# Logits with tokens first from three 16-bit parts, blank entries in order, the first expert tiles' steps earlier, V ahead of the first scores

## The chip, the cores and the metric

The kernel runs on one core of a Trainium2 chip. The metric is the device time of one execution in microseconds; a smaller time is better. A core has a matrix engine (TensorE, PE in the profile, with its weight loads as PEld), VectorE (DVE), ScalarE (ACT), GpSimd (POOL) and SyncE (SP), which here issues DMAs; GpSimd issues DMAs too, the indirect ones among them. Each engine runs its own instructions in order, and they wait for each other by semaphores.

## The reference

Eight batches of attention without softmax, gated by `u`, whose output feeds a mixture of 8 experts, one expert for each token:

```
scores = (1 / S) * z @ z.T                # z: 8 x 2496 x 64
x = u * (max(scores, 0) ** 2 @ v)         # u, v, x: 8 x 2496 x 256
x = x.reshape(19968, 256)
logits = x @ w_gate                       # 256 x 8
e = argmax(logits); gate = softmax(logits)[e]
out = gate * (max(x @ w1[e], 0) @ w2[e])  # w1: 8 x 256 x 1024, w2: 8 x 1024 x 256
```

All data are 32-bit floats, and results must be near those of 32-bit arithmetic.

## The kernel before

**Numbers in parts.** TensorE multiplies in a shorter 32-bit format (`fp32r`). An operand `a` is therefore held as two parts, `hi`, which is `a` copied to that format, and `lo = a - hi`, and a product is three matmuls: hi x hi, hi x lo and lo x hi. The copy is a ScalarE instruction (sometimes VectorE), the subtraction a VectorE one.

**Attention** (`scores`, `weighted`). A batch has 5 chunks of queries (512, the last 448) and 20 blocks of 128 keys, taken in pairs, so that a step `s` is one batch, one chunk and one pair of key blocks: 8 x 5 x 10 = 400 steps. For a step, `scores` makes the 256 x 512 block of squared scores: four matmuls into PSUM (L299, L300), relu and square on ScalarE (L301, L302), then hi (L304) and lo (L306). The score matrix is symmetric, so a block below the diagonal is not computed again: the block above it is turned (L267), written to DRAM as `scr` (L270) and brought back later by four loads (`bring`, L277), at steps that a planner fixes up to `AHEAD = 8` steps ahead of the use. `weighted` then multiplies with V's two parts into two PSUM accumulators: 12 matmuls (L325, L327, L328). `scores` runs `LA = 3` steps ahead of `weighted`. V is loaded by key pair (`fetch_v`, L138) into four buffers and split by `split_v` (ScalarE copy L143, subtraction L145 on VectorE or, in batch 0 from the third pair on, GpSimd). In batch 0 z and V arrive while the first chunk runs.

**After each chunk** (`gate_x`). VectorE forms `x = acc * scale * u` with the 256 features on partitions and tokens along the free side (L350), then hi on ScalarE (L352) and lo on VectorE (L353). Two pieces of work go on the list `bg`, which the main loop takes from, one a step, from the third step of the next chunk on: `logits` and `turn_rows` (x turned to rows and written to DRAM, L365, L370). `logits` has the gate weights as the stationary operand: `wg2` holds for each half of the features 8 columns hi and 8 columns lo, padded to 32, and x streams past, hi and lo, 4 matmuls of 512 columns (L377). Their result has the 32 columns on partitions and tokens along the free side; four 32-row transposes on VectorE (L382) bring tokens to partitions, and `choose` adds the two halves (L405). `route` then picks the expert (`choose`), takes exponentials (`exps`, L401) and finds each token's place among its expert's (`place`: five small 16-bit matmuls L426, L428, then eight VectorE instructions). Four indirect DMAs (L445) scatter entries (gate, token number) into the list `lst` in DRAM, which has a region for each expert.

**Blank entries.** A region is filled with entries that name a pad token before the tokens' own entries come. `blank(b, h)` writes half a batch's share, 624 KB in runs of 768 bytes (L233). Batch 0's two blanks, the regions' ends (L221) and the spare rows (L223) are issued by GpSimd in `constants`; the blanks of batch `b + 1` by SyncE, called at steps 5 and 8 of batch `b`'s second chunk.

**Order.** Instructions are written in program order, but the framework's scheduler may move an instruction ahead on its engine when nothing that it depends on forbids it. `pinned(work)` forbids that: the work's instructions stay behind the last one of each engine at that point. `declare_no_dep` says of two accesses of one DRAM tensor that they touch different places and need not wait for each other.

**Experts.** `tile_list` turns the counts into tiles of 512, 384 or 256 tokens of one expert. Six tiles, the list "A", are built from the counts of the first seven batches, so that they can start while the last batch is routed; the others form the list "F". For a tile, `load_e` fetches its entries (L659), `load_x` its rows (L670), `turn_x` turns them (L700) and passes them through DRAM (`far`, L703, L705), `split_x` makes hi and lo (L715, L716); `load_w` fetches expert weights (L644) and `split_piece` splits them (L689 to L692). `up` and `down` are the two products (L733; L754, L756), and `finish` scatters the result (L767). For the first tiles these calls hang on the last steps of the attention: `loads` names them by their distance from the last step, with `NKP = 10` steps a chunk.

Of the kernel before, what the change touches and what calls it, by code (L numbers as in the profile page):

```python
# [19 lines left out]
P = 128  # L20
# [3 lines left out]
E = 8  # L24
# [24 lines left out]
def fused_kernel(ctx: ExitStack, tc: tile.TileContext, zt, ut, v, wg, wcat, out):  # L49
# [121 lines left out]
    wg2 = const.tile([P, 2, R], FR, name="wg2")  # L171
# [34 lines left out]
    def constants():  # L206
        nc.vector.memset(wg2.bitcast(F32), 0.0)
        nc.vector.tensor_copy(wg2[:, :, 0:E], wg_sb)
        nc.vector.tensor_tensor(wg2[:, :, E:2 * E], wg_sb, wg2[:, :, 0:E].bitcast(F32), op=ALU.subtract)
        for ti, tf in iotas:  # L210
# [7 lines left out]
        blank(0, 0, nc.gpsimd)  # L218
        blank(0, 1, nc.gpsimd)
        w = BIG * ENT // P  # L220
        nc.gpsimd.dma_start(regions[:, NTOK * ENT:].rearrange("e (p k) -> p e k", k=w),  # L221
                            pad[:, 0:w].unsqueeze(1).broadcast_to([P, E, w]))
        nc.gpsimd.dma_start(lst[NROW * SMALL:].rearrange("(p r) k -> p (r k)", p=P), pad[:, 0:w])  # L223

    regions = lst[0:E * CAP].rearrange("(e c) k -> e (c k)", e=E)
    blanks, scatters = [], []

    def blank(b, h, eng=None):
# [4 lines left out]
        i = (eng or nc.sync).dma_start(regions[:, at:at + n * w].rearrange("e (p k) -> p e k", k=w),  # L233
# [108 lines left out]
    def gate_x(b, c, acc):  # L342
# [4 lines left out]
        xh = sb.tile([P, 2, QC], FR, name="xh")  # L347
        xl = sb.tile([P, 2, QC], FR, name="xl")
# [3 lines left out]
        nc.scalar.copy(xh[:, :, :n], x[:, :, :n])  # L352
        nc.vector.tensor_tensor(xl[:, :, :n], x[:, :, :n], xh[:, :, :n].bitcast(F32), op=ALU.subtract)  # L353
# [4 lines left out]
        lw = sb.tile([P, QC // P, R], F32, name="lw", bufs=2)  # L358
        if n < QC:
            nc.gpsimd.memset(lw[n % P:P, ns - 1], 0.0)  # L360
# [11 lines left out]
        def logits():  # L372
            pt = psm.tile([P, QC], F32, name="pt", tag="psm")
            m = 0
            for i in range(2):
                for xx in (xh, xl):
                    nc.tensor.matmul(pt[0:R, :n], lhsT=wg2[:, i], rhs=xx[:, i, :n], start=m == 0, stop=m == 3)  # L377
                    m += 1
            for g in range(G):
                w = -(-(n - g * R) // P)  # L380
                src = pt[0:R].rearrange("p (s g k) -> p g s k", g=G, k=R)[:, g, 0:w]
                nc.vector.transpose(out=lw[g * R:(g + 1) * R, 0:w], in_=src)  # L382
# [3 lines left out]
        lazy.extend(route(b * S + q0, n, ns, lw, gw))  # L386
# [4 lines left out]
    def route(t0, n, ns, lw, gw):  # L391
# [11 lines left out]
        def choose():  # L403
            l = sb.tile(sh, F32, name="l", bufs=2)
            nc.vector.tensor_tensor(l, lw[:, 0:ns, 0:E], lw[:, 0:ns, E:2 * E], op=ALU.add)  # L405
# [14 lines left out]
        def place():  # L420
# [22 lines left out]
            for j in range(ns):  # L443
# [206 lines left out]
    def load_e(i):  # L650
# [7 lines left out]
        for src, at, a, z in parts:  # L658
            nc.gpsimd.indirect_dma_start(out=to[:, a * ENT:z * ENT], out_offset=None, in_=src,  # L659
                                         in_offset=bass.IndirectOffsetOnAxis(ap=eidx[:, at:at + 1], axis=0))  # L660
# [159 lines left out]

    for b in range(B):
        for c in range(NC_):
            s0 = (b * NC_ + c) * NKP
            at(s0 + 2, lambda b=b, c=c: fetch_u(b, c))
            if c == 1 and b + 1 < B:
                for h in range(2):
                    at(s0 + 5 + 3 * h, lambda b=b, h=h: blank(b + 1, h))
# [5 lines left out]
        for kp in range(NKP):  # L833
            if b:
# [162 lines left out]
```

## Time and profile before

| | |
|---|---|
| time, median of 3 runs | 2303.61 us (2300.22 to 2307.38) |
| time of the profiled execution | 2306.15 us |
| its span, first to last instruction | 2304.4 us |
| mean granted TensorE clock | 0.989 |
| busy: TensorE matmuls, VectorE, ScalarE, GpSimd | 97%, 72%, 59%, 29% |
| DMA | 414.28 MB, mean 180 GB/s |

The attention takes the span's first 1364 us, the experts the rest. In the timelines a row gives start, duration, engine, line, operation, tiles (out<-in), shapes and count, and in brackets the idle time of the engine before it with what ended that. In the groups by line a row gives the count, total busy time and mean nanoseconds of one, then the idle time before them. A matmul's duration includes its passage through the array, so matmuls overlap, and the distance of their starts tells their cost.

### The profile page before, as it was taken

The numbers are of one execution on the slowest core, as the hardware profiler recorded it, in microseconds if no ns is written. First come the engines' busy times: TensorE is split into PE (matmuls) and PEld (weight loads), VectorE is DVE, ScalarE is ACT, GpSimd is POOL, SyncE is SP. The second block draws the span as 40 slices with busy tenths as digits, with TensorE's granted clock in tenths as the row PEclk, the third lists the DMA queues.
The fourth block names the chain that finished last, engine by engine and source line by source line (L and its number), as shares of the span: only waits on it lengthen the run. The fifth ranks groups of instructions, "written<-read, shape, count | busy, mean of one in ns | idle before, by whom it ended". The sixth has DMA issues, their size and how long they took to land. (4 is left out here: it accounts for less than half of the span.)

```text
span 2304.4 us, 31091 instructions
## 1 busy us (share of the span) xinstructions
PE 2233.8 (97%) x10864; PEld 1864.5 (81%) x10864; DVE 1653.1 (72%) x2798; ACT 1368.1 (59%) x1818; POOL 673.9 (29%) x724
## 2 busy tenths in 40 slices
PE   5999999999999999999999989999999999999997
PEld 3788788788888888887887878888888888888886
DVE  5687887887887888878878767566566675666653
ACT  4667757857768658667667643454454454554543
POOL 2210020120120120210220344545445555545521
PEclk8999999999999999999999999999999999999999
DMA  8865774775666756657657674555465556556520
GB/s 263 248 183 146 220 191 138 221 178 172 202 162 181 222 141 195 194 142 230 178 129 215 188 225 140 193 166 183 136 200 187 185 186 193 180 164 223 180 87 22
DMA packets 247180, 414.28 MB, mean 180 GB/s; under 512 B 105539, under 2 KB 146056, under 8 KB 227558
## 3 DMA queue, kind: packets, MB, share of 16 engines
q1 hardware_dynamic: 214006, 291.08, 44.1%
q0 software_dynamic: 33008, 121.12, 16.5%
q8 instruction: 87, 1.43, 0.3%
q14 instruction: 79, 0.65, 0.1%
HBM read 254.55 MB, written 158.07 MB: 179 GB/s over the span
## 5 line engine op out<-in xcount | busy, mean ns | idle before, releaser
L325 PE MATMUL acc<-thi,t 128*128 128x512 f32 (+1 forms) x1200 | 453.8, 389 | 23.8 <-ACT t L143 21.2
L328 PE MATMUL acc<-thi,t 128*128 128x512 f32 (+1 forms) x1200 | 462.3, 388 | 0.9 <-POOL t L145 0.5
L445 POOL DMA_INDIRECT lst<-gw,posi x160 | 172.6, 1078 | 963.9 <-DVE posi L442 468.0
L327 PE MATMUL acc<-tlo,t 128*128 128x512 f32 (+1 forms) x1144 | 444.4, 389 | 0.9 <-DVE tlo L306 0.5
L737 ACT ACTIVATE t<-ph 128x512 fp32r<-128x512 f32 (+1 forms) x328 | 192.5, 588 | 342.2 <-PE ph L733 262.0
L733 PE MATMUL ph<-thi,t 128*128 128x512 f32 (+2 forms) x1248 | 377.8, 362 | 14.7 <-ACT thi L715 9.2
L738 DVE SCALAR_TENSOR_TENSOR t<-ph,t 128x512 fp32r<-128x512 f32 (+1 forms) x328 | 220.5, 674 | 229.8 <-ACT t L737 190.6
L754 PE MATMUL y<-t,t 128*128 128x512 f32 x1062 | 379.3, 397 | 1.7 <-DVE tf L765 1.4
L301 ACT ACTIVATE tf<-ps_s 128x1024 f32<-128x1024 f32 (+1 forms) x240 | 242.2, 1017 | 231.5 <-PE ps_s L300 224.5
L756 PE MATMUL y<-t,t 128*128 128x256 f32 x1062 | 290.0, 281 | 2.3 <-DVE t L738 2.3
L325 PEld LDWEIGHTS acc<-thi,t 128*128 128x128 f32 x1200 | 226.3, 189 | 71.3 <-ACT t L143 24.0
L733 PEld LDWEIGHTS ph<-thi,t 128*128 128x128 f32 x1248 | 226.4, 190 | 52.5 <-ACT thi L715 9.3
L328 PEld LDWEIGHTS acc<-thi,t 128*128 128x128 f32 x1200 | 226.8, 189 | 43.9 <-POOL t L145 1.9
L302 ACT ACTIVATE tf<-tf 128x1024 f32<-128x1024 f32 (+1 forms) x240 | 250.4, 1053 | 4.6
L327 PEld LDWEIGHTS acc<-tlo,t 128*128 128x128 f32 x1144 | 216.7, 189 | 42.9 <-DVE tlo L306 3.5
L306 DVE TENSOR_TENSOR tlo<-tf,thi 128x1024 fp32r<-128x1024 f32 (+1 forms) x168 | 203.6, 1215 | 62.0 <-ACT thi L304 59.4
L754 PEld LDWEIGHTS y<-t,t 128*128 128x128 f32 x1062 | 198.0, 188 | 44.7 <-DVE tf L765 1.8
L267 DVE STREAM_TRANSPOSE s<-tf 128x1024 f32<-128x1024 f32 x160 | 197.5, 1235 | 47.1 <-ACT tf L302 42.7
L733 PE MATMUL ph<-tlo,t 128*128 128x512 f32 (+2 forms) x624 | 225.7, 362 | 2.2 <-issue 1.5
L767 POOL DMA_INDIRECT out_dram<-tf,ent x160 | 165.6, 1035 | 184.5 <-DVE tf L765 125.0
L756 PEld LDWEIGHTS y<-t,t 128*128 128x128 f32 x1062 | 200.5, 189 | 14.8 <-DVE t L738 3.7
L670 POOL DMA_INDIRECT rows<-xrows,ent x160 | 164.5, 1028 | 107.5 <-DMA ent<-lst,lfeidx 64.9
(238 smaller groups left out, 3962.7 us busy)
## 6 DMA issues: line engine op xcount, KB each, us to landing
scr<-s SPq DMA_DIRECT2D x80, 1024.0 KB
s<-scr SPq DMA_DIRECT2D x320, 256.0 KB
vr<-in_v_dram SPq DMA_DIRECT2D x80, 256.0 KB
u<-in_ut_dram SPq DMA_DIRECT2D x32, 512.0 KB
xrows<-th SPq DMA_DIRECT2D x128, 128.0 KB
far<-th SPq DMA_DIRECT2D x31, 512.0 KB
th<-far SPq DMA_DIRECT2D x124, 128.0 KB
zr<-in_zt_dram SPq DMA_DIRECT2D x36, 256.0 KB
```

Source lines behind the costliest of these rows:

```text
L267: nc.vector.transpose(out=to, in_=a.rearrange("p i (t s k) -> p i t s k", t=4, s=G))
L301: nc.scalar.activation(a[:, :, :n], ps[:, :, :n], AF.Relu)
L302: nc.scalar.activation(a[:, :, :n], a[:, :, :n], AF.Square)
L306: nc.vector.tensor_tensor(lo[:, :, :n], a[:, :, :n], hi[:, :, :n].bitcast(F32), op=ALU.subtract)
L325: nc.tensor.matmul(acc[d][:, :n], lhsT=vh, rhs=hi[:, i, :n], start=first and i == 0, stop=False)
L327: nc.tensor.matmul(acc[d][:, :n], lhsT=vh, rhs=lo[:, i, :n], start=False, stop=False)
L328: nc.tensor.matmul(acc[d][:, :n], lhsT=vl, rhs=hi[:, i, :n], start=False, stop=last and i == 1)
L733: nc.tensor.matmul(o, lhsT=w1[:, part, dd, fs], rhs=xx[:, dd, :n], start=p == 0, stop=p == 5)
L737: nc.scalar.activation(hh[:, :m], ph[:, :m], AF.Relu)
L738: nc.vector.scalar_tensor_tensor(hl[:, :m], ph[:, :m], 0.0, hh[:, :m].bitcast(F32), op0=ALU.max, op1=ALU.subtract)
L754: nc.tensor.matmul(y, lhsT=hh[:, cs], rhs=w2[:, f % 2].rearrange("p i d -> p (i d)"), start=f == 0, stop=False)
L756: nc.tensor.matmul(y[:, 0:D], lhsT=hl[:, cs], rhs=w2[:, f % 2, 0, :], start=False, stop=f == NF - 1)
```

## The change

Four parts.

1. **Logits.** x is split into three 16-bit parts that sum to it: the upper halves of x's 32-bit words, read in place at every second 16-bit element (`tops[0]`), the upper halves of what remains (`x1`, `tops[1]`), and the rest of that as a 16-bit tile (`x2`). Both subtractions are VectorE's; ScalarE's copy is gone. The parts are the stationary operand, 128 tokens at a time, and the gate weights in three 16-bit parts side by side (24 columns) stream past. A chunk has 4 blocks of tokens x 2 halves of the features x 3 parts = 24 matmuls, whose result has tokens on partitions; one VectorE sum over the three weight parts (two for a chunk of 448) gives `l`. The transposes, `lw` and the addition in `choose` are gone.
2. **Blanks.** All are issued by SyncE and pinned: batch 0's at steps 6 and 7, the regions' ends and spare rows (`tails`) at step 8, the later ones at the places where they were called.
3. **First expert tiles.** Entry loads of the list "A" and the scatters of the last batch are declared free of each other, and the first tiles' calls are moved: `load_e(0)`, `load_e(1)`, `load_x(0)`, `load_e(2)`, `load_x(1)` and `turn_x(0)` by 4, 4, 2, 8, 4 and 3 steps.
4. **V in the first chunk.** The split of the next key pair's V is emitted ahead of `scores` of three steps later, instead of behind it.

```diff
     def constants():
-        nc.vector.memset(wg2.bitcast(F32), 0.0)
-        nc.vector.tensor_copy(wg2[:, :, 0:E], wg_sb)
-        nc.vector.tensor_tensor(wg2[:, :, E:2 * E], wg_sb, wg2[:, :, 0:E].bitcast(F32), op=ALU.subtract)
+        for k in range(3):
+            nc.vector.tensor_copy(wg3[:, :, k, :], wg_sb)
+            if k < 2:
+                nc.vector.tensor_tensor(wg_sb, wg_sb, wg3[:, :, k, :], op=ALU.subtract)
...
-        blank(0, 0, nc.gpsimd)
-        blank(0, 1, nc.gpsimd)
+
+    def tails():
+
         w = BIG * ENT // P
-        nc.gpsimd.dma_start(regions[:, NTOK * ENT:].rearrange("e (p k) -> p e k", k=w),
-                            pad[:, 0:w].unsqueeze(1).broadcast_to([P, E, w]))
-        nc.gpsimd.dma_start(lst[NROW * SMALL:].rearrange("(p r) k -> p (r k)", p=P), pad[:, 0:w])
+        nc.sync.dma_start(regions[:, NTOK * ENT:].rearrange("e (p k) -> p e k", k=w),
+                          pad[:, 0:w].unsqueeze(1).broadcast_to([P, E, w]))
+        nc.sync.dma_start(lst[NROW * SMALL:].rearrange("(p r) k -> p (r k)", p=P), pad[:, 0:w])
...
-        xh = sb.tile([P, 2, QC], FR, name="xh")
-        xl = sb.tile([P, 2, QC], FR, name="xl")
+        x1 = sb.tile([P, 2, QC], F32, name="x1")
+        x2 = sb.tile([P, 2, QC], BF16, name="x2")
+        tops = [t.bitcast(BF16).rearrange("p i (n h) -> p i n h", h=2)[:, :, :, 1] for t in (x, x1)]
...
-        nc.scalar.copy(xh[:, :, :n], x[:, :, :n])
-        nc.vector.tensor_tensor(xl[:, :, :n], x[:, :, :n], xh[:, :, :n].bitcast(F32), op=ALU.subtract)
+        nc.vector.tensor_tensor(x1[:, :, :n], x[:, :, :n], tops[0][:, :, :n], op=ALU.subtract)
+        nc.vector.tensor_tensor(x2[:, :, :n], x1[:, :, :n], tops[1][:, :, :n], op=ALU.subtract)
...
         def logits():
             pt = psm.tile([P, QC], F32, name="pt", tag="psm")
-            m = 0
-            for i in range(2):
-                for xx in (xh, xl):
-                    nc.tensor.matmul(pt[0:R, :n], lhsT=wg2[:, i], rhs=xx[:, i, :n], start=m == 0, stop=m == 3)
-                    m += 1
-            for g in range(G):
-                w = -(-(n - g * R) // P)
-                src = pt[0:R].rearrange("p (s g k) -> p g s k", g=G, k=R)[:, g, 0:w]
-                nc.vector.transpose(out=lw[g * R:(g + 1) * R, 0:w], in_=src)
+            W = 3 * E
+            for t in range(ns):
+                m = min(P, n - t * P)
+                for i in range(2):
+                    for xx in (*tops, x2):
+                        nc.tensor.matmul(pt[:m, t * W:(t + 1) * W], lhsT=xx[:, i, t * P:t * P + m],
+                                         rhs=wg3[:, i].rearrange("p k e -> p (k e)"),
+                                         start=t == 0 and i == 0 and xx is tops[0],
+                                         stop=t == ns - 1 and i == 1 and xx is x2, skip_group_check=True)
+            sums = pt[:, 0:ns * W].rearrange("p (t k e) -> p t e k", k=3, e=E)
+            full = n // P
+            nc.vector.tensor_reduce(l[:, 0:full], sums[:, 0:full], axis=AX.X, op=ALU.add)
+            if full < ns:
+                nc.vector.tensor_reduce(l[:n % P, full], sums[:n % P, full], axis=AX.X, op=ALU.add)
...
         def choose():
-            l = sb.tile(sh, F32, name="l", bufs=2)
-            nc.vector.tensor_tensor(l, lw[:, 0:ns, 0:E], lw[:, 0:ns, E:2 * E], op=ALU.add)
...
+                for o in firsts:
+                    tc.declare_no_dep(i.ins, o.ins, reason="places of an earlier batch")
...
+            if which == "A":
+                firsts.append(d)
+                for of, o in scatters:
+                    if of == B - 1:
+                        tc.declare_no_dep(d.ins, o.ins, reason="places of a later batch")
...
+    for h in range(2):
+        at(6 + h, lambda h=h: pinned(lambda: blank(0, h)))
+    at(8, lambda: pinned(tails))
...
-                    at(s0 + 5 + 3 * h, lambda b=b, h=h: blank(b + 1, h))
+                    at(s0 + 5 + 3 * h, lambda b=b, h=h: pinned(lambda: blank(b + 1, h)))
...
-    loads = {NKP + 4: [lambda: load_e(0)],
-             NKP + 3: [lambda: load_e(1)],
-             NKP + 2: [lambda: load_x(0)],
+    loads = {2 * NKP - 2: [lambda: load_e(0)],
+             2 * NKP - 3: [lambda: load_e(1)],
+             NKP + 4: [lambda: load_x(0)],
+             NKP + 3: [lambda: load_e(2)],
              NKP + 1: [lambda: load_w(0, 0)],
+             NKP: [lambda: load_x(1)],
              NKP - 1: [lambda: load_w(0, 1)],
              NKP - 3: [lambda: load_w(1, 0)],
-             NKP - 4: [lambda: load_x(1)],
-             NKP - 5: [lambda: turn_x(0), lambda: load_e(2)],
+             NKP - 2: [lambda: turn_x(0)],
              1: [lambda: load_x(2), lambda: load_e(3)],
              0: [lambda: turn_x(1)]}
...
+        if s < NKP and kp + 1 < NKP:
+            pinned(lambda: split_v(0, kp + 1))
         if s + LA <= LAST:
             ready[s + LA] = scores(*steps[s + LA])
-        if s < NKP:
-            if kp + 1 < NKP:
-                pinned(lambda: split_v(0, kp + 1))
-            if kp % 2 == 0 and kp // 2 + 2 < NC_:
-                pinned(lambda: split_z(0, kp // 2 + 2))
+        if s < NKP and kp % 2 == 0 and kp // 2 + 2 < NC_:
+            pinned(lambda: split_z(0, kp // 2 + 2))
```

More of the change, by code (lines that the diff above doesn't have):

```diff
@@ L170, in fused_kernel @@
     make_identity(nc, ident)
-    wg2 = const.tile([P, 2, R], FR, name="wg2")
+    wg3 = const.tile([P, 2, 3, E], BF16, name="wg3")
     wg_sb = const.tile([P, 2, E], F32, name="wg_sb")
@@ L217, in constants, with blank @@
         nc.gpsimd.iota(pad.bitcast(I32)[:, 1:PAD * ENT:ENT], pattern=[[0, PAD]], base=NTOK, channel_multiplier=0)
-        blank(0, 0, nc.gpsimd)
-        blank(0, 1, nc.gpsimd)
+    def tails():
         w = BIG * ENT // P
-        nc.gpsimd.dma_start(regions[:, NTOK * ENT:].rearrange("e (p k) -> p e k", k=w),
-                            pad[:, 0:w].unsqueeze(1).broadcast_to([P, E, w]))
-        nc.gpsimd.dma_start(lst[NROW * SMALL:].rearrange("(p r) k -> p (r k)", p=P), pad[:, 0:w])
+        nc.sync.dma_start(regions[:, NTOK * ENT:].rearrange("e (p k) -> p e k", k=w),
+                          pad[:, 0:w].unsqueeze(1).broadcast_to([P, E, w]))
+        nc.sync.dma_start(lst[NROW * SMALL:].rearrange("(p r) k -> p (r k)", p=P), pad[:, 0:w])
     regions = lst[0:E * CAP].rearrange("(e c) k -> e (c k)", e=E)
-    blanks, scatters = [], []
-    def blank(b, h, eng=None):
+    blanks, scatters, firsts = [], [], []
+    def blank(b, h):
         w, n = PAD * ENT, S // PAD // 2
@@ L232, in blank @@
         at = (b * S + h * S // 2) * ENT
-        i = (eng or nc.sync).dma_start(regions[:, at:at + n * w].rearrange("e (p k) -> p e k", k=w),
+        i = nc.sync.dma_start(regions[:, at:at + n * w].rearrange("e (p k) -> p e k", k=w),
                                        pad[0:n].unsqueeze(1).broadcast_to([n, E, w]))
@@ L357, in gate_x @@
         nc.gpsimd.iota(gw.bitcast(I32)[:, 0:ns, 1], pattern=[[P, ns]], base=b * S + q0, channel_multiplier=1)
-        lw = sb.tile([P, QC // P, R], F32, name="lw", bufs=2)
+        l = sb.tile([P, ns, E], F32, name="l", bufs=2)
         if n < QC:
-            nc.gpsimd.memset(lw[n % P:P, ns - 1], 0.0)
+            nc.gpsimd.memset(l[n % P:P, ns - 1], 0.0)
         def turn_rows():
@@ L373, in logits, with route @@
             pt = psm.tile([P, QC], F32, name="pt", tag="psm")
-            m = 0
-            for i in range(2):
-                for xx in (xh, xl):
-                    nc.tensor.matmul(pt[0:R, :n], lhsT=wg2[:, i], rhs=xx[:, i, :n], start=m == 0, stop=m == 3)
-                    m += 1
-            for g in range(G):
-                w = -(-(n - g * R) // P)
-                src = pt[0:R].rearrange("p (s g k) -> p g s k", g=G, k=R)[:, g, 0:w]
-                nc.vector.transpose(out=lw[g * R:(g + 1) * R, 0:w], in_=src)
+            W = 3 * E
[12 more added lines that the diff above has]
+                nc.vector.tensor_reduce(l[:n % P, full], sums[:n % P, full], axis=AX.X, op=ALU.add)
         bg.append(logits)
         bg.append(turn_rows)
-        lazy.extend(route(b * S + q0, n, ns, lw, gw))
+        lazy.extend(route(b * S + q0, n, ns, l, gw))
     def nothing():
         pass
-    def route(t0, n, ns, lw, gw):
+    def route(t0, n, ns, l, gw):
         mlast = n - (ns - 1) * P
@@ L658, in load_e @@
         for src, at, a, z in parts:
-            nc.gpsimd.indirect_dma_start(out=to[:, a * ENT:z * ENT], out_offset=None, in_=src,
-                                         in_offset=bass.IndirectOffsetOnAxis(ap=eidx[:, at:at + 1], axis=0))
+            d = nc.gpsimd.indirect_dma_start(out=to[:, a * ENT:z * ENT], out_offset=None, in_=src,
+                                             in_offset=bass.IndirectOffsetOnAxis(ap=eidx[:, at:at + 1], axis=0))
+            if which == "A":
[3 more added lines that the diff above has]
+                        tc.declare_no_dep(d.ins, o.ins, reason="places of a later batch")
     def token(i, s):
```

## The prediction

> **What bounds it now.** I read the windows first, then who made TensorE wait, then the timelines of the two places where it waits. A window's row gives its length, the busy time (and number) of TensorE, its weight loads, VectorE, ScalarE and GpSimd, then the granted clock, the DMA share and GB/s.
>
> ```profile
> 0.00:100.00 100.00, 71.20 (x248) 50.13 (x249) 55.48 (x66) 57.10 (x64) 23.92 (x39) 0.86 0.92 273
> 100.00:1200.00 1100.00, 1095.71 (x5040) 903.55 (x5039) 893.47 (x1487) 755.60 (x817) 155.23 (x207) 1.00 0.64 180
> ```
> ```profile
> PE acc L325 <- ACT t L143: 21.2, 5, 12.7
> PE ph L733 <- ACT thi L715: 9.2, 1, 9.2
> PE ps_s L299 <- ACT tf L301: 2.2, 3, 1.6
> ```
>
> From 100 to 1200 us TensorE lacks only 4.3 us: the attention is bound by it, so a microsecond of matrix work added or removed there is one of time, while VectorE and ScalarE have room. Its large waits stand in two places: 21.2 us on the copies of V at the start (the last row is from the first 100 us alone) and 9.2 us on the first expert tile's split. So the change has three terms: start, turn to the experts, logits.
>
> **The start.** TensorE, SyncE's queue and ScalarE, in the first 60 us:
>
> ```profile
> 4.98 1.19 PE L299 MATMUL ps_s<-t 128*128 128x512 f32 x2
> 12.87 0.79 PE L325 MATMUL acc<-thi,t 128*128 128x512 f32 x2 [2.52 <-ACT thi L304]
> 19.18 0.50 PE L325 MATMUL acc<-thi,t 128*128 128x512 f32 x1 [1.25 <-ACT t L143]
> 27.36 0.80 PE L325 MATMUL acc<-thi,t 128*128 128x512 f32 x1 [2.57 <-ACT t L143]
> 40.80 0.79 PE L325 MATMUL acc<-thi,t 128*128 128x512 f32 x1 [4.46 <-ACT t L143]
> 45.78 0.63 PE L327 MATMUL acc<-tlo,t 128*128 128x512 f32 x1
> 46.20 0.63 PE L328 MATMUL acc<-thi,t 128*128 128x512 f32 x1
> 59.51 0.80 PE L325 MATMUL acc<-thi,t 128*128 128x512 f32 x1 [12.68 <-ACT t L143]
> ```
> ```profile
> 8.96 38.51 SPq L233 DMA_DIRECT2D lst<-pad  x14
> 49.67 1.55 SPq L138 DMA_DIRECT2D vr<-in_v_dram  x1
> ```
> ```profile
> lst<-pad SPq DMA_DIRECT2D x14, 624.0 KB
> ```
> ```profile
> 23.93 1.94 ACT L301 ACTIVATE tf<-ps_s 128x1024 f32<-128x1024 f32 x2 [4.80 <-PE ps_s L300]
> 58.84 0.62 ACT L143 CAST t<-vr 128x512 fp32r<-128x512 f32 x1 [17.15 <-DMA vr<-in_v_dram]
> ```
> ```profile
> 111.05 0.39 PE L325 MATMUL acc<-thi,t 128*128 128x512 f32 x1
> ...
> 111.96 0.19 PE L426 MATMUL pr<-oh,tri 128*128 128x32 bf16 x1
> 112.00 0.24 PE L428 MATMUL pr<-oh,ones 128*128 128x32 bf16 x4
> 112.10 0.47 PE L327 MATMUL acc<-tlo,t 128*128 128x512 f32 x1
> 112.41 0.39 PE L328 MATMUL acc<-thi,t 128*128 128x512 f32 x1
> ```
>
> All 14 blanks of batches 1 to 7 went out at once, as soon as the pad was there, and held SyncE's queue from 8.96 to 47.5 us; the sixth load of V came behind them, and TensorE waited 12.68 us. The 1.25, 2.57 and 4.46 us have another cause: ScalarE's copy of V stood behind the next scores' relu, which waited 4.80 us for TensorE, which waited for that copy. After long waits the clock is halved too: 45.78 to 46.20 is 0.42 us a matmul, where the four from 111.05 to 111.96 (three are left out) take 0.91, 0.227 each.
>
> How short can the first 100 us become? 248 matmuls less the 8 that warm up, times 0.227, are 54.5. What stays: 5.0 to the first score, 2.5 for the first weights and some 10 matmuls at half clock after it (2.0), 2.2 of the waits on relu: 66. For the DMA: 100 us at 273 GB/s are 27.3 MB; 14 blanks of 624 KB (8.9 MB) leave, 18.4 MB at the same rate are 67. Both floors nearly coincide, and batch 0's two blanks and the tails now stand on SyncE's queue at steps 6 to 8, ahead of what that queue still has to issue: a ninth V, score rows written and brought back, u. A blank held the queue 38.51/14 = 2.75 us, three of them 8.3. I take 74, **a gain of 26**. Upper end: 34 (66 reached). Lower end: 15, the 12.68 us alone with its eleven matmuls at half clock (2.2). V's copy ahead of the scores has a price: where V has not landed, ScalarE's relus wait behind it; with the queue free, four V buffers are filled ahead, so I count none beyond the 8 us between 66 and 74.
>
> The 14 blanks come back two to a batch, steps 5 and 8 of the second chunk, pinned on SyncE's queue. Queued behind them are loads of turned scores, planned up to 8 steps early, 8 x 12 x 0.227 = 22 us, against 2.75; DMA is 0.64 busy there. Cost nought; without that cover 14 x 2.75 = 38. GpSimd loses four DMA issues, off the path.
>
> **The turn to the experts.**
>
> ```profile
> 1351.12 1.20 DVE L700 STREAM_TRANSPOSE th<-rows 128x1024 f32<-128x1024 f32 x1
> ```
> ```profile
> 1354.03 0.46 SPq L703 DMA_DIRECT2D far<-th  x1
> 1361.21 1.78 SPq L705 DMA_DIRECT2D th<-far  x4
> ```
> ```profile
> 1373.24 1.65 PE L733 MATMUL ph<-thi,t 128*128 128x512 f32 x3 [9.20 <-ACT thi L715]
> 1374.68 0.63 PE L733 MATMUL ph<-tlo,t 128*128 128x512 f32 x1
> 1375.11 1.05 PE L733 MATMUL ph<-thi,t 128*128 128x512 f32 x2
> ```
> ```profile
> 1340.00:1350.00 10.00, 10.00 (x51) 8.83 (x50) 6.82 (x11) 7.22 (x9) 4.64 (x4) 1.00 0.60 194
> 1360.00:1370.00 10.00, 4.04 (x25) 3.48 (x23) 7.05 (x20) 3.23 (x6) 1.46 (x2) 0.92 1.00 324
> ```
>
> The first tile's turn starts at 1351, lies 7 us in a write to DRAM, and its read back meets full DMA (1.00). The change emits that turn three steps earlier; a step here is 12 matmuls of 448 columns, 12 x 0.2 = 2.4 us, so 7 us, into DMA at 0.60. Both legs then pass before the weight loads: the 9.2 us go, and about 13 matmuls at half clock (0.43 instead of 0.227: 2.6). **A gain of 10**; ends 3 and 12. The earlier entry loads lose their wait for batch 7's scatters; that only moves GpSimd's queue. What is late next: the second tile's turn, needed only a whole tile later.
>
> **The logits.**
>
> ```profile
> 129.44 0.40 PE L377 MATMUL pt<-xh,wg 128*32 128x512 f32 x1
> 129.68 0.40 PE L377 MATMUL pt<-xl,wg 128*32 128x512 f32 x1
> ```
> ```profile
> 111.97 0.17 PEld L428 LDWEIGHTS <-ones 128*128 128x128 bf16 x4
> ```
> ```profile
> L733 PEld LDWEIGHTS ph<-thi,t 128*128 128x128 f32 x1248 | 226.4, 190 | 52.5 <-ACT thi L715 9.3 <-DVE t L738 7.6
> L377 PEld LDWEIGHTS pt<-xl,wg 128*32 128x32 f32 x80 | 8.6, 108 | 9.0 <-issue 0.2
> L428 PEld LDWEIGHTS <-ones 128*128 128x128 bf16 x160 | 7.0, 97 | 0.0
> L353 DVE TENSOR_TENSOR xl<-x,xh 128x1024 fp32r<-128x1024 f32 (+1 forms) x40 | 47.6, 1191 | 0.0
> L382 DVE STREAM_TRANSPOSE lw<-pt 32x128 f32<-32x128 f32 (+1 forms) x160 | 47.8, 299 | 24.8 <-issue 16.1 <-PE pt L377 7.0
> ```
> ```profile
> 122.90 1.22 DVE L353 TENSOR_TENSOR xl<-x,xh 128x1024 fp32r<-128x1024 f32 x1
> ```
>
> Out go 160 matmuls at 0.235 (129.44 to 129.68), a fifth of them of 448 columns at 7/8 of that: 36.6 us. In come 24 for each of 40 chunks, 960, each with a stationary of its own: 128 tokens of 16-bit x, 24 columns moving. Nearest row: the routing's five small ones, each with a dense 16-bit 128x128 load. Four loads span 0.17 with 0.097 for one: a step of 0.025. The next large matmul then loses its hidden load (112.10 to 112.41 is 0.31 instead of 0.227), 0.1 once. A chunk costs 24 x 0.025 + 0.1 = 0.7, all 28: **a gain of 9**. What no row shows: two of three parts are read at every second 16-bit place, since they are the upper halves of 32-bit words. Ends: 0.025, and the 32-bit load without its fixed part: (190 - 108)/96 columns = 0.85 ns a column, 0.11 for 128. I take 0.025, because type and shape are the nearest row's and 16 bits already load far faster than that (128 columns in 97 ns, 32 columns of 32 bits in 108).
>
> The Trainium skill, "TensorE: Matmul & The Clock Gate", section on weight-path perf modes, says two things: 16-bit loads of 128 columns take a fast path, with column steps up to 1,024 elements allowed; and that path gains by reading 32 bits at a time, two bf16, with no win for fp32. By the first the strided parts cost what the dense do, as I take it; by the second a 32-bit word holds one useful half and the win may go, which is the second rival below.
>
> VectorE loses L353 and L382, 95 us, and L405's 40 small adds; it gains two subtractions like L353, also 95, and 40 sums of 96 numbers from PSUM that take the adds' place, longer than one and surely shorter than a 1.2 us operation: 0 to 48 more. ScalarE loses 40 copies. Neither shows where TensorE lacks 4.3 of 1100 us and VectorE is busy 893. The chain to the logits grows by one subtraction, 1.2 us; in the second chunk L353 ended at 124.1 and the logits began at 129.44, 5.3 us later, two steps into the next chunk. Bare, it would be 40 x 1.2 = 48.
>
> **Sum.** The profiled execution took 2306.15 (span 2304.4), 2.5 above the median of 2303.61. 2306.15 - 26 - 10 - 9 = 2261; on the median's footing **2259**. Its own range, from the ends of start and turn: 2249 to 2277.
>
> **Rivals.** *The start stays DMA-bound or queue-bound*: V comes in time, but turned scores and batch 0's blanks keep TensorE waiting; gain 15 instead of 26, turn 3: 2277. For it, DMA share 0.92; against, a third of those bytes leaves. *The strided loads are slow* (the slower side): TensorE, at each chunk's logits. 16 loads at 0.11 plus 24 columns of moving (0.01), nothing hidden: 16 x 0.12 + 8 x 0.025 + 0.1 = 2.2 a chunk, 88 in all, 51 more than before instead of 9 less: 2319. It decides at about 0.095 us a load, where 640 loads and the 12 us of the rest eat up the 36.6 us that the old logits free and the 36 of start and turn; faster by less than 0.3% from 0.084, slower by more from 0.106. *The change is not carried out*, the scheduler still sending blanks or the turn where they were: start 8 (the reordered V alone), turn 0: 2286; against it, the blanks are pinned.
>
> **Chances.** Forecast 0.63, start bound 0.13, strided loads slow 0.17, not carried out 0.07. 0.3% is 7 us, what a measurement can tell. The range leaves out the slow loads alone: 2245 (2249, and the 0.1 us of the lost hidden load not paid 40 times) to 2288 (past the 2286 above; it holds the forecast with all loads at 0.045 too, 19 us more, 2278). Slow loads are likelier at 0.11 to 0.12, slower, than at 0.085 to 0.105, no change. Faster 0.83, same 0.06, slower 0.11.
>
> **What would show it.** Right: no wait over 2 us on L143 after 13 us; blanks on SyncE's queue spread, two to a batch; TensorE busy some 80 of the first 100 us instead of 71, without half clock after 20 us; no long wait before the first L733; new logits 25 ns apart; attention's TensorE idle still under 1%. Wrong: strided loads 50 ns apart or more, a new wait of TensorE at chunk starts, a halved clock anywhere in the attention.

## The result, and the profile after

The changed kernel took 2260.83 us (median of 5 runs, 2258.57 to 2262.16) beside 2303.27 us for the kernel before (5 runs, 2300.22 to 2307.38): a ratio of 0.9817, 95% interval 0.9804 to 0.9831, 42 us less. The forecast was 2259. The profiled execution took 2262.16, its span 2260.4.

The same views as before, of the changed kernel. The windows first:

```profile
0.00:100.00 100.00, 86.49 (x359) 64.96 (x360) 72.99 (x98) 67.02 (x75) 24.76 (x39) 0.93 0.74 225
100.00:1200.00 1100.00, 1097.19 (x5746) 913.50 (x5745) 903.10 (x1393) 737.18 (x794) 160.71 (x207) 1.00 0.67 189
```

TensorE is busy 86.49 of the first 100 us instead of 71.20, and issues 359 matmuls there (24 of them the small ones of the new logits) instead of 248, at a DMA share of 0.74 instead of 0.92. The attention after that is still TensorE's. Its waits:

```profile
PE acc L327 <- ACT t L143: 7.9, 3, 4.5
PE ph L746 <- DVE t L751: 3.8, 3, 2.9
PE ps_s L301 <- ACT tf L303: 3.0, 4, 0.8
```

The waits for V's copies (L143) fell from 21.2 to 7.9 us, and the 9.2 us ahead of the first up product are off the list. What is left of the start, in TensorE's timeline and in two windows (rows as in the prediction: length, busy times of the engines, then granted clock, DMA share and GB/s):

```profile
28.28 0.50 PE L327 MATMUL acc<-s,t 128*128 128x512 f32 x1 [2.56 <-ACT t L143]
42.39 0.79 PE L327 MATMUL acc<-thi,t 128*128 128x512 f32 x1 [4.46 <-ACT t L143]
```
```profile
30.00:40.00 10.00, 7.93 (x28) 6.01 (x26) 5.20 (x7) 3.72 (x6) 2.41 (x2) 0.83 0.87 262
40.00:50.00 10.00, 7.43 (x22) 5.51 (x23) 8.97 (x7) 3.98 (x6) 4.16 (x3) 0.66 0.86 257
```

The 12.68 us went. Waits of 2.56 and 4.46 us are there, as long as two that the forecast wanted gone (the first experiment shows that they stand one key pair further on), and the granted clock in these two windows is 0.83 and 0.66. SyncE's queue:

```profile
18.36 0.33 SPq L138 DMA_DIRECT2D vr<-in_v_dram  x1
...
56.13 0.41 SPq L235 DMA_DIRECT2D lst<-pad  x1
...
249.69 2.73 SPq L235 DMA_DIRECT2D lst<-pad  x1
256.02 0.45 SPq L235 DMA_DIRECT2D lst<-pad  x1
```

V's sixth load goes out at 18.36 instead of 49.67, and the blanks come two to a batch. The turn to the experts (VectorE, SyncE, TensorE):

```profile
1295.17 1.20 DVE L713 STREAM_TRANSPOSE th<-rows 128x1024 f32<-128x1024 f32 x1
```
```profile
1299.96 2.04 SPq L716 DMA_DIRECT2D far<-th  x1
1306.70 1.94 SPq L718 DMA_DIRECT2D th<-far  x4
```
```profile
1336.16 0.36 PE L330 MATMUL acc<-s,t 128*128 128x448 f32 x1
1336.36 0.39 PE L746 MATMUL ph<-thi,t 128*128 128x512 f32 x1
```

The first tile's turn runs 41 us ahead of its use, and the first up product follows the last weighted matmul by 0.20 us. The new logits, in TensorE's timeline and in the groups by line (count, total and mean ns):

```profile
80.07 0.72 PE L382 MATMUL pt<-wg,x 128*128 128x24 bf16 x22
80.64 0.48 PE L329 MATMUL acc<-tlo,t 128*128 128x512 f32 x1
80.95 0.39 PE L330 MATMUL acc<-thi,t 128*128 128x512 f32 x1
```
```profile
L382 PEld LDWEIGHTS <-x 128*128 128x128 bf16 x960 | 29.1, 97 | 15.0 <-issue 12.7 <-DVE s L308 0.8 <-DVE t L751 0.3
L434 PEld LDWEIGHTS <-ones 128*128 128x128 bf16 x160 | 7.0, 97 | 0.0
```

The 22 here (two went before, between other work) take 80.07 to 80.64, 0.57 us, and the next large matmul takes 0.31 instead of 0.227. The row of the new logits' loads, of which two in three are at every second 16-bit place, and that of the routing's dense loads have the same mean, 97 ns.

To see where the time went, the span is cut at four marks that every run has: the end of the first chunk (VectorE's first `x<-acc`), the attention's last weighted matmul, the matmul behind a gap of 0.74 us some 142 us into the experts, and the end. The marks of the kernel before and then of the changed one, as far as they aren't shown above:

```profile
88.29 1.29 DVE L350 SCALAR_TENSOR_TENSOR x<-acc,u 128x512 f32<-128x512 f32 x2 [0.64 <-PE acc L328]
```
```profile
1363.55 0.37 PE L328 MATMUL acc<-s,t 128*128 128x448 f32 x1
```
```profile
1521.09 0.50 PE L733 MATMUL ph<-tlo,t 128*128 128x512 f32 x1 [0.74 <-issue]
```
```profile
66.96 1.25 DVE L353 SCALAR_TENSOR_TENSOR x<-acc,u 128x512 f32<-128x512 f32 x2
```
```profile
1478.31 0.50 PE L746 MATMUL ph<-tlo,t 128*128 128x512 f32 x1 [0.74 <-issue]
```

| us | to the first chunk's end | to the last weighted matmul | to the 0.74 us gap | to the end |
|---|---|---|---|---|
| before | 88.29 | 1275.26 | 157.54 | 783.35 |
| changed | 66.96 | 1269.20 | 142.15 | 782.14 |
| less | 21.3 | 6.1 | 15.4 | 1.2 |

The sum, 44.0, is the difference of the spans.

### The profile page after: what moved, and what is told of

It is laid out like the page before. It is cut to its first block, busy times and chain, and to the rows that moved or that the text cites. A ratio compares the mean times of both kernels' runs of the same rounds, so it can differ in the third digit from the quotient of the medians.

```text
span 2260.4 us, 32529 instructions
## 1 busy us (share of the span) xinstructions
PE 2219.2 (98%) x11664; PEld 1866.3 (83%) x11664; DVE 1653.6 (73%) x2688; ACT 1334.2 (59%) x1778; POOL 678.3 (30%) x720
## 4 chain that ended last, share of the span: by engine, by line
PE 84%; issue 6%; DVE 3%; DMA 3%; ACT 2%; POOL 1%; SPq 0%; POOLq 0%; DVEq 0%; another core or an unknown queue 0%; ACTq 0%
PE ph L746 16%; PE acc L330 14%; PE acc L327 14%; PE acc L329 14%; PE y L767 11%; PE y L769 6%; PE ps_s L301 4%; PE ps_s L302 4%; DMA scr<-s 1%; PE pt L382 1%; POOL out_dram L780 1%; DMA xrows<-th 1%; ACT tf L303 1%; ACT thi L306 0%; DVE tlo L308 0%
## 5 line engine op out<-in xcount | busy, mean ns | idle before, releaser
L451 POOL DMA_INDIRECT lst<-gw,posi x160 | 182.0, 1138 | 901.2 <-DVE posi L448 822.5
L303 ACT ACTIVATE tf<-ps_s 128x1024 f32<-128x1024 f32 (+1 forms) x240 | 242.2, 1018 | 236.3 <-PE ps_s L302 225.7
```

What stands on the lines that cost most here:

```text
L303: nc.scalar.activation(a[:, :, :n], ps[:, :, :n], AF.Relu)
```

## The experiments

Theory: three terms that add, with two causes at the start, the blanks that hold SyncE's queue and V's copy behind the relus. Rivals: one part makes nearly all of it, or the parts stand in for each other. The runs were made in four groups, each beside the kernel before on the same chip (its medians 2298.66, 2300.18, 2304.91 and 2303.88), so ratios compare across groups and microseconds within one.

### V's split behind the scores again (part 4 undone)

```diff
-        if s < NKP and kp + 1 < NKP:
-            pinned(lambda: split_v(0, kp + 1))
         if s + LA <= LAST:
             ready[s + LA] = scores(*steps[s + LA])
+        if s < NKP and kp + 1 < NKP:
+            pinned(lambda: split_v(0, kp + 1))
```

> The changed kernel with one part undone: V's split emitted behind the scores again. Theory (the start gains because the blanks left SyncE's queue): the emitted order of V does not decide, 2261 us within 3, and the waits on L143 stay 7.9 us in three. Rival (the reordered V brought part of the start's gain): the waits of 1.25 and 2.57 us before the third and fourth weights return with their half clock, 2266 to 2269 us.

Measured: 2262.89 us (2260.37 to 2267.05), ratio 0.9856 (0.9836 to 0.9877). The first chunk ends at 72.32, 5.4 later; the attention's last weighted matmul comes at 1339.89, 3.7 later. TensorE's timeline of this run:

```profile
19.44 0.50 PE L327 MATMUL acc<-thi,t 128*128 128x512 f32 x1 [1.08 <-ACT t L143]
...
27.63 0.76 PE L327 MATMUL acc<-thi,t 128*128 128x512 f32 x1 [2.57 <-ACT t L143]
41.24 0.71 PE L327 MATMUL acc<-thi,t 128*128 128x512 f32 x1 [4.46 <-ACT t L143]
...
46.02 0.39 PE L327 MATMUL acc<-thi,t 128*128 128x512 f32 x1
```

The first is back, near the 1.25 us of before; part 4 had removed it. The other two have the same lengths as with part 4, and from 24 to 44 us ScalarE does the same things in the same order in both runs, but they are waits for other V. Counted in the two timelines, 24 weighted matmuls stand ahead of the wait of 2.57 us and 48 ahead of the 4.46 us here, as in the kernel before; in the changed kernel it is 36 and 60. A key pair has 12, so each wait stands one key pair further on there. That is what part 4 brings: the 61st weighted matmul starts at 46.02 here and at 42.39 in the changed kernel, 3.6 of the 5.4 us. The rest of the difference comes later, in the chunk's second half.

The ratio lies 0.004 above the changed kernel's, some 9 us, but the span of the profiled execution, 2259.1 us, is shorter than the changed kernel's 2260.4: from the 0.74 us gap to the end it takes 777.4 us instead of 782.1 (more on this stage below). The theory's time, 2261 us within 3, was met, and its reason was not: the order of V does decide 5.4 us at the start.

### The later blanks free to go out early (a half of part 2 undone)

```diff
-                    at(s0 + 5 + 3 * h, lambda b=b, h=h: pinned(lambda: blank(b + 1, h)))
+                    at(s0 + 5 + 3 * h, lambda b=b, h=h: blank(b + 1, h))
```

> The changed kernel with the 14 later blanks no longer pinned; batch 0's two and the tails stay where the change put them. Theory (queue): the 14 go out together early, hold SyncE's queue some 38 us, a load of V lands late again and TensorE waits over 10 us on L143: the whole start gain of 21 us is lost, 2278 to 2284 us. Rival (V order and batch 0's blanks carry half of it): 2270 us. Second rival (it is the bytes, not the queue): no single long wait, but DMA at 0.9 for 60 us and 2268 to 2275 us.

Measured: 2263.12 us (2257.4 to 2265.28), ratio 0.9848 (0.9826 to 0.987). SyncE's queue in this run:

```profile
8.97 28.98 SPq L235 DMA_DIRECT2D lst<-pad  x14
```

The blanks went out at 9 us as before and held the queue, but to 38 us, not to 47.5. The longest wait for V is 6.71 us instead of 12.68, and the first chunk ends at 70.27, 3.3 later: far less than expected. The 14 blanks on SyncE's queue by themselves do not explain the start.

### The old logits (part 1 undone)

The edit puts back the removed lines of part 1 of the diff above (`wg2`, `xh`, `xl`, `lw`, the four matmuls and the transposes) and takes out the added ones.

> The changed kernel with the old logits (gate weights stationary in two 32-bit parts, copy on ScalarE, four transposes on VectorE). Theory: TensorE's 40 x (0.94 - 0.75) us come back, 2268 us (2266 to 2270). Rival (the relief of VectorE or ScalarE, or the shorter use of the PSUM tile, is what counted): over 2272 us with new waits of TensorE in the attention. Second rival (logits are hidden): 2261 us.

Measured: 2267.63 us (2264.43 to 2269.93), ratio 0.9867 (0.985 to 0.9884). From the first chunk's end to the last weighted matmul it takes 1277.12 us, 7.9 more than the changed kernel. The expected 2268 us came. The window of this run shows that most of it is work, not waiting:

```profile
100.00:1200.00 1100.00, 1095.67 (x5036) 903.67 (x5036) 895.43 (x1477) 762.94 (x826) 153.50 (x207) 1.00 0.68 188
```

TensorE is nearly as full as in the changed kernel, 1095.67 instead of 1097.19 us; it only gets less of the attention done in 1100 us. Over the whole stretch between the two marks it idles 4.4 us here and 2.8 us in the changed kernel, so 6.3 of the 7.9 us are work and 1.6 are waiting.

### The old turn to the experts (part 3 undone)

```diff
-    loads = {2 * NKP - 2: [lambda: load_e(0)],
-             2 * NKP - 3: [lambda: load_e(1)],
-             NKP + 4: [lambda: load_x(0)],
-             NKP + 3: [lambda: load_e(2)],
+    loads = {NKP + 4: [lambda: load_e(0)],
+             NKP + 3: [lambda: load_e(1)],
+             NKP + 2: [lambda: load_x(0)],
              NKP + 1: [lambda: load_w(0, 0)],
-             NKP: [lambda: load_x(1)],
              NKP - 1: [lambda: load_w(0, 1)],
              NKP - 3: [lambda: load_w(1, 0)],
-             NKP - 2: [lambda: turn_x(0)],
+             NKP - 4: [lambda: load_x(1)],
+             NKP - 5: [lambda: turn_x(0), lambda: load_e(2)],
```

The two accesses declared free of each other are taken back as well.

> The changed kernel with the first expert tiles' calls at their old places and without the new declarations between entry loads and scatters. Theory: the wait before the first up product (9 us) and its half clock (2.6 us) return, 2272 us (2270 to 2275). Rival (the expert phase gained 7 us in all, so the turn brought more than that wait): 2276 us or more. Second rival (with the rest of the change the old places are early enough): 2263 us or less.

Measured: 2267.22 us (2266.02 to 2273.88), ratio 0.9879 (0.9857 to 0.9901). TensorE's waits and the first 10 us of the experts in this run:

```profile
PE ph L741 <- ACT thi L723: 6.9, 1, 6.9
```
```profile
1343.18:1353.00 9.82, 9.82 (x56) 7.76 (x57) 4.91 (x10) 1.79 (x3) 4.71 (x5) 0.78 0.22 58
```

The wait is back with 6.9 us, then the clock is 0.78. From the last weighted matmul to the 0.74 us gap it takes 151.81 us; the changed kernel takes 142.15, and 141.75 in a second profile. The turn costs 9.7 to 10.1 us there; how much of it the earlier calls bring and how much the declarations, no run separates. But the rest of the experts took 777.14 instead of 782.14, so only 4.3 us are left at the end of the span (by the ratios of the runs it is 0.006, some 14 us). The timelines show where those 5 us are: first the changed kernel, then this place of the run with V's split behind. The run with the old turn has no idle time of TensorE there either (busy 10.00 of the 10 us from 2152, at a clock of 1.00).

```profile
2145.90 0.50 PE L746 MATMUL ph<-thi,t 128*128 128x512 f32 x1 [2.91 <-DVE t L751]
```
```profile
2143.00:2153.00 10.00, 10.00 (x59) 8.66 (x59) 9.12 (x17) 6.31 (x12) 4.36 (x5) 1.00 0.81 251
```

Some 807 us into the experts one up product waits for VectorE in some runs (3.33 us in the kernel before, 2.91 in the changed kernel) and not in others (no idle time in the second row); a lower clock follows it, 0.83 from 2143 to 2153 us in the changed kernel. It is not the only such wait: over all runs the last stage takes 776.6 to 785.1 us, whatever was changed, and the run with the 785.1 (z's split sooner) does not have this one. So a few microseconds won earlier are not always to be seen at the end, and the parts are better compared at the marks.

### The changed kernel again

Unaltered, to stand beside the next three on one chip.

> The changed kernel once more, unaltered, on the chip of the runs beside it, so that they can be set against it: 2258 to 2262 us, first chunk's last weighted matmul at 65 us of the span.

Measured: 2258.72 us (2256.05 to 2264.21), ratio 0.9816 (0.9784 to 0.9847). First chunk's end 66.61.

### The first batch's blanks and the tails on GpSimd (the other half of part 2 undone)

```diff
+        blank(0, 0, nc.gpsimd)
+        blank(0, 1, nc.gpsimd)
...
-        nc.sync.dma_start(regions[:, NTOK * ENT:].rearrange("e (p k) -> p e k", k=w),
+        nc.gpsimd.dma_start(regions[:, NTOK * ENT:].rearrange("e (p k) -> p e k", k=w),
...
-        nc.sync.dma_start(lst[NROW * SMALL:].rearrange("(p r) k -> p (r k)", p=P), pad[:, 0:w])
+        nc.gpsimd.dma_start(lst[NROW * SMALL:].rearrange("(p r) k -> p (r k)", p=P), pad[:, 0:w])
...
-    for h in range(2):
-        at(6 + h, lambda h=h: pinned(lambda: blank(0, h)))
-    at(8, lambda: pinned(tails))
```

> The first batch's two blanks and the tails back on GpSimd's queue (1.5 MB ahead of everything else there, from 9 us on); later blanks still in order, V's split still ahead of the scores. Theory that parts 2 and 4 each remove the same delay: V's copy stays ahead of the relus, only bandwidth is lost for the 1.5 MB, 2 to 5 us: 2263 us. Rival, that GpSimd's blanks were the weight on the first 50 us: first chunk's end at 80 us or later, 2275 us.

Measured: 2258.09 us (2256.05 to 2261.11), ratio 0.9814 (0.9782 to 0.9846); first chunk's end 66.09. These 1.5 MB by themselves cost nothing that these runs can tell; neither the theory's 2 to 5 us nor the rival's 80 us for the first chunk came.

### Part 2 wholly undone, part 4 kept

The edits of the two runs above together (`blank` of batch 0 and the tails on GpSimd, the later blanks not pinned).

> Part 2 wholly undone (first batch's blanks on GpSimd, the 14 later ones free to go out at 9 us), part 4 kept. Theory that parts 2 and 4 each suffice for the order of V's copy and the relus: wait of the weighted matmuls for V(5) near 10 us, first chunk's end at 70 us, 2265 us. Rival, that the blanks' jam of the queues and the DMA engines is what the start costs: first chunk's end at 80 us or later, 2275 to 2281 us.

Measured: 2270.01 us (2267.87 to 2272.58), ratio 0.9872 (0.9839 to 0.9904), 11.3 more than the changed kernel beside it; first chunk's end 78.86, 12.3 later. SyncE's queue, GpSimd's and TensorE:

```profile
8.98 38.18 SPq L234 DMA_DIRECT2D lst<-pad  x14
47.26 1.95 SPq L138 DMA_DIRECT2D vr<-in_v_dram  x1
```
```profile
9.27 2.14 POOL L234 DMA_DIRECT2D lst<-pad  x2 [0.31 <-POOL pad L218]
```
```profile
28.13 0.50 PE L326 MATMUL acc<-s,t 128*128 128x512 f32 x1 [2.56 <-ACT t L143]
55.27 0.79 PE L326 MATMUL acc<-thi,t 128*128 128x512 f32 x1 [17.50 <-ACT t L143]
```

With GpSimd's two at the same time, the 14 hold SyncE's queue 38 us instead of 29; V's next load goes out at 47.26, and TensorE waits 17.50 us. The two halves of part 2 do not add: singly they cost the first chunk 3.3 to 3.7 and -0.9 to -0.5 us (against the two profiles of the changed kernel), together 11.9 to 12.3. The theory's 70 us was too low; the rival's 80, from the jam, was nearly right.

### Parts 2 and 4 both undone

The edits of the last run and of the first.

> Parts 2 and 4 both undone: the start of the kernel before with the new logits and the new turn. Both theories: V's copies behind the relus and V(5) late, first chunk's end at 85 us, 20 us over the changed kernel: 2281 us. If it comes out at 2265 us, neither part made the start's gain, and the logits' or the turn's code did by where it puts the instructions.

Measured: 2278.62 us (2273.81 to 2279.8), ratio 0.9902 (0.9868 to 0.9935), 19.9 more than the changed kernel beside it; first chunk's end 86.50, 19.9 later, the last weighted matmul 18.3 later. The start's gain is made by these two parts. By the first chunk's end:

| us | blanks in order | blanks early, on both queues |
|---|---|---|
| V's split ahead | 66.6 | 78.9 |
| V's split behind | 72.3 | 86.5 |

The blanks' order is worth 12 to 14 us, V's place 5 to 8 (4 to 6 by the last weighted matmul). The theory that either of the two parts would do by itself falls.

### z's split sooner; V two key pairs ahead; both

What is left of the start was looked for in three variants of the changed kernel. In the first, the split of z's next chunk moves ahead of V's split and the scores:

```diff
+        if s < NKP and kp % 2 == 0 and kp // 2 + 2 < NC_:
+            pinned(lambda: split_z(0, kp // 2 + 2))
         if s < NKP and kp + 1 < NKP:
             pinned(lambda: split_v(0, kp + 1))
         if s + LA <= LAST:
             ready[s + LA] = scores(*steps[s + LA])
-        if s < NKP and kp % 2 == 0 and kp // 2 + 2 < NC_:
-            pinned(lambda: split_z(0, kp // 2 + 2))
```

> The changed kernel, with the split of z's next key chunk recorded ahead of V's split and of the next scores, not behind them. Theory that what is left of the start's waits comes from z's split, which stands on VectorE behind the low parts of the scores before it (the scores come in pairs, some 12 us apart, and ScalarE waits 5 to 6 us for them): pairs closer, half clock between 30 and 50 us gone, first chunk's end at 58 us instead of 65, 2252 us. Rival, that V's copy behind the relus sets it: no change, 2259 us.

Measured: 2261.14 us (2260.25 to 2265.82), ratio 0.9822 (0.9794 to 0.985). ScalarE's relus (L303) in the changed kernel and then in this one:

```profile
24.84 1.94 ACT L303 ACTIVATE tf<-ps_s 128x1024 f32<-128x1024 f32 x2 [5.29 <-PE ps_s L302]
37.06 1.94 ACT L303 ACTIVATE tf<-ps_s 128x1024 f32<-128x1024 f32 x2 [6.28 <-PE ps_s L302]
49.83 1.94 ACT L303 ACTIVATE tf<-ps_s 128x1024 f32<-128x1024 f32 x2 [6.02 <-PE ps_s L302]
```
```profile
20.61 1.94 ACT L303 ACTIVATE tf<-ps_s 128x1024 f32<-128x1024 f32 x2 [1.08 <-PE ps_s L302]
32.43 1.94 ACT L303 ACTIVATE tf<-ps_s 128x1024 f32<-128x1024 f32 x2 [5.86 <-PE ps_s L302]
44.98 1.94 ACT L303 ACTIVATE tf<-ps_s 128x1024 f32<-128x1024 f32 x2 [5.81 <-PE ps_s L302]
```

The theory holds for the first pair of scores, whose wait shrinks by 4.2 us; the later pairs stay some 12 us apart. Of TensorE's waits for V's copy the one of 2.56 us goes and the one of 4.46 us stays. The first chunk ends at 62.11, 4.5 to 4.9 sooner, and the last weighted matmul comes 4.5 to 4.9 sooner as well. In the span that is 1.9 us less than in the changed kernel's first profile and 4.0 less than in its second; the medians don't show it.

In the second, V is split a pair earlier:

```diff
+    split_v(0, 1)
...
-        if s < NKP and kp + 1 < NKP:
-            pinned(lambda: split_v(0, kp + 1))
+        if s < NKP and kp + 2 < NKP:
+            pinned(lambda: split_v(0, kp + 2))
```

> The changed kernel, with V split two key tiles ahead of its use instead of one. Rival theory (V's copy behind the relus): the two waits of the weighted matmuls for V, 2.6 and 4.5 us, go, first chunk's end at 59 us, 2253 us. Theory that z's split sets the pace: PE waits for the scores instead, no change, 2259 us; V's tiles not landed yet would hold ScalarE up, so a loss of some us is possible.

Measured: 2271.62 us (2270.5 to 2276.27), ratio 0.9867 (0.9839 to 0.9895); first chunk's end 69.86, 2.9 to 3.3 later, and 2.8 more in the attention. Its waits in the first 100 us:

```profile
PE acc L327 <- ACT t L143: 6.2, 2, 4.5
PE acc L329 <- DVE tlo L308: 4.0, 3, 2.0
```

The 4.5 us wait stays, again one key pair further on (72 weighted matmuls stand ahead of it, 60 in the changed kernel), and a new one for the low parts of the scores comes. The reading that V's copy behind the relus sets the start falls with its 59 us. The other reading allowed for a loss, and a loss it is, but not by V landing late: no instruction of ScalarE waits for a load of V in the first 75 us.

The third has both edits.

> Both: z's split ahead of the scores and V's two tiles ahead. If each theory holds a part, the sum: first chunk's end near 55 us, 2249 us. If DMA sets the pace (V's and z's tiles not landed), no more than either alone.

Measured: 2262.34 us (2258.83 to 2263.62), ratio 0.9822 (0.9796 to 0.9848); first chunk's end 62.05, as with z's split alone, and 2.0 us more in the attention. None of the three beats the changed kernel (0.9816, 0.9817) in the time of the runs.

### The later blanks early, but on GpSimd

```diff
+        for bb in range(1, B):
+            for hh in range(2):
+                blank(bb, hh, nc.gpsimd)
...
-            if c == 1 and b + 1 < B:
-                for h in range(2):
-                    at(s0 + 5 + 3 * h, lambda b=b, h=h: pinned(lambda: blank(b + 1, h)))
```

> The changed kernel, with the 14 later blanks issued by GpSimd at 9 us instead of by SyncE two to a batch: the same 8.9 MB go out in the first 50 us as in the kernel before, but SyncE's queue stays free of them. Theory that the jam of SyncE's queue is the price of early blanks: V(5) issued near 29 to 33 us, first chunk's end at 65 to 69 us (GpSimd spends some 15 us on issuing, up to 5 of them ahead of its first low part of V), 2259 to 2263 us. Rival, that the bytes are the price whoever issues them: V's and the score rows' transfers land late, first chunk's end at 77 us or later, 2270 us or more.

Measured: 2279.98 us (2278.18 to 2282.18), ratio 0.9892 (0.9869 to 0.9915); first chunk's end 87.68. GpSimd and TensorE's waits in the first 100 us:

```profile
8.69 8.42 POOL L238 DMA_DIRECT2D lst<-pad  x9 [0.31 <-POOL pad L218]
20.38 0.91 POOL L238 DMA_DIRECT2D lst<-pad  x1 [3.27 <-DMA lst<-pad]
...
44.48 0.91 POOL L238 DMA_DIRECT2D lst<-pad  x1 [11.97 <-DMA lst<-pad]
45.41 1.27 POOL L145 TENSOR_TENSOR t<-vr,t 128x512 fp32r<-128x512 f32 x1
```
```profile
PE acc L333 <- POOL t L145: 23.7, 3, 22.4
```

GpSimd issued nine, then had to wait for one to land before each further one; its low part of V (L145) came behind the last, at 45.41, and TensorE waited 22.4 us for that. The jam moved to the engine that issues. So the time fits the rival, but not for the rival's reason, transfers that land late: the price was again an instruction that stands behind the issues. Whether the same 8.9 MB would cost anything from an engine with nothing else to do was not tried.

## Why the prediction was right, and where it was not

**The sum** was right, 45 us forecast and 44.0 found between the spans. That it came so near is partly luck: the start gave 5 to 8 us less than its term and the logits 1 less, while 5 to 6 us in the turn's stage and 1.2 in the last stage came that no term held.

**The start** was to give 26. Undoing parts 2 and 4 takes 19.9 us at the first chunk's end and 18.3 at the end of the attention: inside the term's ends (15 to 34), 6 to 8 below its value. By the forecast's own measure it is 19.0: the kernel before starts 248 large matmuls in its first 100 us, and the changed kernel starts its 248th at 80.95 (the row is shown above), where 74 had been forecast. Both causes are real: the blanks' order 12 to 14 us (12.68 and 2.2 of half clock had been named as the lower end), V's place 5 to 8. That the latter is near the sum of the 1.25, 2.57 and 4.46 us is luck, since of these three only the 1.25 went.

The step that failed is that the change ends these waits. The circle that the prediction read behind them is right: V's copy stands behind the next scores' relus, they wait for TensorE, and TensorE for the copy. Part 4 moves the copy ahead by one key pair, and the circle closes again there: in the changed kernel the scores come in pairs some 12 us apart (the relus at 24.84, 37.06 and 49.83), and the copies that TensorE waits for, at 27.62 and 41.71, still follow the relus of such a pair. z's split accounts for 4.2 us of the first pair's wait; what would end the later ones was not found. With those waits stayed the half clock between 30 and 50 us, which the prediction had named as a sign of being wrong. So "no wait over 2 us on L143 after 13 us" and "without half clock after 20 us" were wrong and "two to a batch" right; TensorE is busy 86 of the first 100 us, more than the "some 80". That V's copy ahead of the scores would cost nothing held: no copy of V on ScalarE waits for its load in the first 75 us.

**The blanks' cost in the middle**, nought: no run separates it, but the attention's TensorE lacks 2.8 of 1100 us, less than before.

**The turn** was to give 10. Undone alone it takes 9.7 to 10.1 us: 7.2 between the last weighted matmul and the first up product and the rest in the first tile, at a clock of 0.78; the forecast had items of 9.2 and 2.6 and shortened their sum to 10. Against the kernel before, the stage lost 15.4. The 5 to 6 us between were not forecast. The wait was 9.2 there and 6.9 with the new logits; and the kernel before has, in its window of 10 us at 1425, VectorE busy 9.93 and two waits of TensorE for it, 1.7 us in all, which no later run has. The runs at hand narrow this down. The stage takes 157.5 us in the kernel before, with old logits and old turn, 151.8 with the old turn alone, 141.5 with the old logits alone, and 141.8 with the old start alone. So these 5 to 6 us stand only where the old logits and the old turn meet. That it is the old logits' VectorE work in the last chunks is argued, not shown.

```profile
1425.00:1435.00 10.00, 8.25 (x39) 6.25 (x38) 9.93 (x37) 2.94 (x6) 3.94 (x4) 1.00 0.29 93
```

**The logits** were to give 9, and gave 7.9 by the run that undoes them, 6.3 of it work. The disputed size was right: a load at every second 16-bit place takes 97 ns as a dense one does, and the matmuls follow each other at 25 ns. The Trainium skill's "TensorE: Matmul & The Clock Gate", section on weight-path perf modes, says two things of this; the one on column steps holds here, and the reading by which half of each 32-bit word goes to waste does not. The Trainium skill's "TensorE: Matmul & The Clock Gate", section "Wait — 56ns, not 53.3ns?", says that starts never come closer than about 25 ns. The trace agrees: the 22 above take 0.57 us, 26 ns each.

The term lacked two things. In 19 of the 32 full chunks the 24 matmuls go in two or three pieces, as the 22 and 2 above, and each piece costs the large matmul behind it some 0.09 us, where the term had counted 0.1 once a chunk. The second are the chunks of 448 tokens, whose last block is 64 columns wide. TensorE's timeline of one of them:

```profile
201.43 0.90 PE L382 MATMUL pt<-wg,x 128*128 128x24 bf16 x24
202.26 0.50 PE L301 MATMUL ps_s<-t,t 128*128 128x512 f32 x1
202.60 0.39 PE L302 MATMUL ps_s<-t,t 128*128 128x512 f32 x1
```

It takes 0.83 us plus 0.11 of the next matmul (0.34 instead of 0.23), so 0.94 where 0.7 had been counted. The old logits of such a chunk took 4 x 0.235 x 7/8 = 0.82 us: eight of the 40 chunks lose a little instead of saving. In the trace the starts of the 18 full ones stand 25 ns apart, but for the first, and the first of the six narrow ones 102 ns behind them. The Trainium skill's "TensorE: Matmul & The Clock Gate", section on weight-path perf modes, lists a full 128 columns among the fast load's conditions. The trace agrees: the loads of 64 columns take 107 to 113 ns, those of 128 columns 97.

**The last stage** was not spoken of. It moved by -1.2 us here and by up to 8.5 from run to run, through waits that come or not. A time within 2 us of the forecast is partly luck for that reason too.

**The rivals.** The strided loads were not slow, and the change was carried out. *The start stays bound* has its truth in the start's 18 to 21 us instead of 26, but the turn came in whole.

## What to carry to other kernels

A transfer that nobody needs yet is not free: here the engine that issued 14 of them was held up by them, and the price is the instruction behind them, 12 us for V's loads on SyncE (3 without the 1.5 MB beside them) and 21 us for V's low part when GpSimd issued instead. When the same wait appears in the trace to the hundredth of a microsecond, ask what holds the instructions ahead of it before counting it as gone: moving V's copy ahead by one key pair moved two of its three waits by one key pair, and did not end them. Small matmuls with a 16-bit stationary operand can take it from the halves of 32-bit words in place, here at no cost as long as a block has its 128 columns. Cut a sum at marks that every run has, since the end of the span mixes in waits that come and go.

## What the runs showed of the hardware

- Fourteen blanks of 624 KB held SyncE's queue 29.0 us by themselves and 38.2 us beside 1.5 MB more on GpSimd's queue (38.5 in the kernel before, 37.2 with parts 2 and 4 undone): 9 us more with 18% more bytes.
- GpSimd issued nine of these DMAs in 8.42 us, and then each of the other five only once an earlier one had landed, the last at 44.48 us.
- Loads of 128 x 128 16-bit columns take 97 ns dense or at every second place; the first of the loads of 64 columns behind them takes 107 ns, and its matmul starts 102 ns after the one before it, where full blocks start 25 ns apart.
- A wait of 2.9 us in the experts is there in some runs and not in others, though the edits lie 800 us or more ahead of it, and a lower clock follows it (0.83 over 10 us).
